# Three empty places in the order of the attention units of an attention-and-FFN kernel

## The chip, the core and the metric

One core of one Trainium2 chip runs the whole program. The metric is the device time of one execution in microseconds (us); the figure that counts is the median of several runs. Five engines work side by side, each in the order of its own instruction stream: PE (TensorE, matrix products; PEld is its loading of weights), DVE (VectorE), ACT (ScalarE), POOL (GpSimd) and SP (SyncE, which here only issues transfers). They wait for one another through semaphores, and a waiting instruction holds up everything behind it on its engine.

## What is computed

Causal attention in a window of 128 positions, with a linear bias for each head, for 8 batches of 8 heads, 576 positions and head size 64; and on its result, taken as 4608 tokens of 512 values, a feed-forward network with a sigmoid gate.

```python
scores = scale * np.matmul(q, k.transpose(0, 1, 3, 2))
scores = np.where(mask, scores + bias[None], -1000000000.0)
attn = np.exp(scores - np.max(scores, axis=-1, keepdims=True))
attn = attn / (np.sum(attn, axis=-1, keepdims=True) + 1e-09)
x = np.matmul(attn, v).transpose(0, 2, 1, 3).reshape(B * S, H * D)
h = x @ w_in
g = h * (1.0 / (1.0 + np.exp(-1.702 * h)))
return g @ w_out
```

## The kernel before

**Attention** is cut into units of one pair of heads and up to 256 queries. Batches 0 and 1 are cut "whole": three sections of 256, 256 and 64 queries, each with four units, one for a pair of heads. That makes 12 units for each of these two batches. Batches 2 to 7 have 20 units each, of a finer form. The list `units` holds all of them in order, and a *tick* moves the pipeline on by one place: in tick n the unit at place n gets its scores (`scores`, PE, L324 for the whole units), the one at n-1 its bias and minimum (`biased`, DVE, L351), its exponents (`exponents`, ACT, L374) and its normalization (`normal`, DVE L392 and L393 for the reciprocal, then L402 on POOL or DVE and L399 on ACT), the one at n-2 its transposition (`flip`, PE L419 and copies on ACT and DVE, L427), and the one at n-3 its product with v (`mix`, PE L476, copied out at L485 into the tile of tokens `x` or `xf`). A tick also loads a later unit's q and k through SP.

**The FFN** works on chunks of 256 tokens, 18 of them, each in 16 steps, one for each 128 of the 2048 hidden values. A step is `up` (12 products into `h_ps`, L552: the high part `xh` of the tokens with both parts of the weights, then the low part `xl` with the high part), a chain over ACT (L557, tanh), DVE (L558), ACT (L561, `gh`) and POOL (L562, `gl`), and `down` (6 products into `acc`, L571). Chunk 0 runs its first 8 steps, then chunk 1 its 16, then chunk 0 the rest, then chunks 2 to 17. At the start of a chunk `split_x` (L536, L538) makes `xh` on ACT and `xl` half on POOL and half on DVE.

**The weights** come as 64-bit words and are decoded once, in 32 halves (a `w_in` and a `w_out` half for each of the 16 steps): L211 on ACT, L212 and L213 on DVE, L216 on ACT for the high part, L217 on POOL for the low part. All of it happens beside the first FFN steps. In the names below `w_7_925` is a decoded half of step 7: the smaller last number is its `w_in` half.

**What sets the order.** The first 7 ticks run before the first FFN step. After that a planner in the main loop gives each FFN step a share of a tick: for each entry of `due` (so many units must be done when such a chunk begins) it divides the ticks still to go by the steps still to go, and takes the largest quotient (`pace`). Chunk 0 starts at step 0, chunk 1 at step 8, chunk 2 at step 32. In the kernel before, `due` begins with 4, 8, 12 and 16 units for the chunks 0, 1, 2 and 2 (chunk 2 holds the last 64 tokens of batch 0 and the first 192 of batch 1). Over the program order that comes of this, a scheduler then sets each engine's stream by its own simulated times, so an instruction can stand earlier or later on its engine than the loop wrote it.

The units that the change touches are the third section of batch 0 (64 queries, `64x192` in the rows), at places 8 to 11, and what follows them, the first section of batch 1 (`128x128` and `128x256` in the rows).

Of the kernel before, what the change touches and what calls it, by code (L numbers as in the profile page):

```python
# [32 lines left out]
BIG = 3.0e38  # L33
FAR = 1.0e37
DEPTH = 3
BESIDE = range(4)
WB = 2
DECODE_TICKS = 5, 6, 7
# [65 lines left out]
def whole_batch(b):  # L104
    units = []
    for hp in range(NP):
        blocks = pair_blocks(hp)
        n = len(blocks)
        chunks = [Chunk(i * P, P, [(blocks[i], P)] + [(z, 0) for z in blocks[i + 1:i + 2]]) for i in range(n)]
        for i in range(0, n, 3):  # L110
            Segment(i * P, 3 * P, P if i + 3 < n else 0, chunks[i:i + 3])
        done = 0
        for i in range(0, n, 2):
            upto = min(i + 1, n) if i + 2 < n else n
            units.append(Unit(b * NP + hp, blocks[i:i + 2], chunks[i:i + 2], chunks[done:upto]))
            done = upto
    return units
# [20 lines left out]
def part_batch(b, lo, hi):  # L138
    return [WholeUnit(b, hp, lo, hi) for hp in range(NP)]
# [3 lines left out]
def tile_kernel(ctx: ExitStack, tc: tile.TileContext, q0, k0, v0, qT, kT, v, w_in, w_out, out):  # L143
# [103 lines left out]
    def load_whole(u):  # L247
        if u.at == DEPTH:

            u.rq = ffn.tile([P, 2 * P], F32, name="rq", tag="g")  # L250
            u.rk = ffn.tile([P, 2 * P], F32, name="rk", tag="gh")
            u.rv = ffn.tile([P, 2, 2, D], F32, name="VV", tag="gl")
        else:
            u.rq = raw.tile([P, 2 * P], F32, name="rq", tag="rq")
            u.rk = raw.tile([P, 3 * P], F32, name="rk", tag="rk")
        move(u.rq[:, :u.hi - u.lo], q0[u.pair, :, u.lo:u.hi])
        if u.early:
            tc.keep_in_program_order(nc.scalar.dma_start(u.rk[:, :u.hi - u.k0], k0[u.pair, :, u.k0:u.hi]))
        else:
            move(u.rk[:, :u.hi - u.k0], k0[u.pair, :, u.k0:u.hi])  # L260

    def load_whole_v(u):
        if u.at != DEPTH:
            u.rv = att.tile([P, 3, 2, D], F32, name="VV", bufs=3)
        full = (u.hi - u.k0) // P
        end = u.k0 + full * P
        move(u.rv[:, :full], v0[u.pair, u.k0:end].rearrange("(c p) h d -> p c h d", p=P))
        if end < u.hi:
            move(u.rv[:u.hi - end, full], v0[u.pair, end:u.hi])
# [262 lines left out]
    def split_x(c, x):  # L532
        xh = xp.tile([P, NC, T], F32R, name="xh")
        xl = xp.tile([P, NC, T], F32R, name="xl")
        for k in range(NC):
            (nc.scalar.copy if c in BESIDE else nc.vector.tensor_copy)(xh[:, k], x[:, k])  # L536
            sub = nc.vector if k % 2 else nc.gpsimd
# [54 lines left out]
    units, due = [], []  # L592
    for b in range(B):
        start = max((b * S + S - 1) // T - XBUFS, 0)
        if b < WB:
            for lo, hi in ((0, 2 * P), (2 * P, 4 * P), (4 * P, S)):
                units += part_batch(b, lo, hi)
                due.append((len(units), (b * S + lo) // T, start))
        else:
            units += whole_batch(b)  # L600
            due.append((len(units), b * S // T, start))
    for n, u in enumerate(units):
        u.at = n
        u.early = n < due[0][0]
    units += [None] * 4
    loads = [u for u in units if u]
    ticks = 0
# [115 lines left out]
def build(nc, arrays):  # L723
    args = []
    for name, a in arrays.items():
        args.append(nc.dram_tensor(name, a.shape, mybir.dt.from_np(a.dtype), kind="ExternalInput").ap())
    args.append(nc.dram_tensor("out", (NT, DM), F32, kind="ExternalOutput").ap())
    with tile.TileContext(nc, schedule_with_timeline_sim=True) as tc:
        tile_kernel(tc, *args)
# [44 lines left out]
```

## Time and profile before

| | |
|---|---|
| median of 3 runs | 1064.5 us (1063.76 to 1065.91) |
| the profiled execution | 1068.36 us |
| its span, from the first to the last instruction | 1066.3 us |
| mean granted PE clock over the span | 0.995 of full speed |
| moved from and to HBM | 67.63 MB read, 9.44 MB written, 72 GB/s over the span |
| chain of work that ended last, by engine | PE 94%, DVE 3%, ACT 1%, DMA 1%, issue 1% |

The span is cut into stretches below; "busy" is the time in which an engine worked on an instruction, and a row with a number in brackets at its end tells how long the engine had stood idle before the instruction, and what it had waited for. A PE product is counted busy until its result is out, so two products that follow each other closely overlap: what a product costs PE is the distance between starts, which is smaller than its duration.

### The profile page before, as it was taken

What the parts mean: (1) busy time and instruction counts of PE and PEld (TensorE: products, weight loads), DVE (VectorE), ACT (ScalarE), POOL (GpSimd) and SP (SyncE); (2) the same over time, 40 slices, a digit from 0 to 9 for tenths busy, and PEclk for the clock granted to TensorE, in tenths of its full rate; (3) what the DMA queues carried; (4) which work ended last, traced back from release to release, by engine and by line L of the source; (5) the groups of instructions that cost most, each with busy time, mean ns of one, the idle gap of its engine ahead of it and who ended that gap; (6) DMA issues with size and microseconds to landing.
All of it is one profiled execution on the core that took longest, in us unless ns stands there. A gap on an engine that the chain in (4) does not pass through costs nothing.

```text
span 1066.3 us, 21362 instructions
## 1 busy us (share of the span) xinstructions
PE 1052.9 (99%) x7041; PEld 929.1 (87%) x7041; DVE 660.5 (62%) x2117; ACT 597.2 (56%) x1811; POOL 603.5 (57%) x863
## 2 busy tenths in 40 slices
PE   9899999999999999999999999999999999999998
PEld 5567787889989999999999999999999999998987
DVE  6797522568887777545767668767877687313121
ACT  6879853466666565535555556655665656322222
POOL 4579933567676666554656557656666665323232
PEclk9899999999999999999999999999999999999999
DMA  8872001223222132102121223212222221000000
GB/s 307 281 261 73 25 22 56 73 67 96 75 76 81 51 102 67 57 14 71 54 79 52 71 62 91 66 60 78 79 63 85 57 78 28 20 2 20 1 21 20
DMA packets 88109, 78.45 MB, mean 74 GB/s; under 512 B 36800, under 2 KB 79296, under 8 KB 88000
## 3 DMA queue, kind: packets, MB, share of 16 engines
q1 hardware_dynamic: 82240, 67.14, 21.4%
q10 hardware_dynamic: 5760, 9.96, 2.6%
q8 instruction: 55, 0.90, 0.3%
q14 instruction: 54, 0.44, 0.1%
HBM read 67.63 MB, written 9.44 MB: 72 GB/s over the span
## 4 chain that ended last, share of the span: by engine, by line
PE 94%; DVE 3%; ACT 1%; DMA 1%; issue 1%; POOL 0%; SPq 0%; DVEq 0%; POOLq 0%; ACTq 0%
PE h_ps L552 38%; PE acc L571 37%; PE s_ps L334 5%; PE x_ps L499 5%; PE t_ps L442 4%; PE x_ps L476 2%; PE t_ps L419 1%; PE sb_ps L324 1%; PE s_ps L324 1%; DVE wc L213 1%; DMA rw<-w_out 1%; ACT pb L374 1%; DVE rec L392 0%; PE acc L189 0%; DVE rw L212 0%
## 5 line engine op out<-in xcount | busy, mean ns | idle before, releaser
L562 POOL TENSOR_TENSOR gl<-g,gh 128x256 fp32r<-128x256 f32 x288 | 218.0, 757 | 292.2 <-ACT gh L561 224.9
L552 PE MATMUL h_ps<-xh,w 128*128 128x256 f32 x2304 | 370.2, 284 | 1.1 <-POOL w L217 0.6
L552 PEld LDWEIGHTS h_ps<-xh,w 128*128 128x128 f32 x2304 | 328.5, 189 | 34.5 <-issue 2.8
L571 PE MATMUL acc<-w,gh 128*128 128x512 f32 x1152 | 324.9, 400 | 0.0
L558 DVE SCALAR_TENSOR_TENSOR g<-g,h_ps 128x256 f32<-128x256 f32 x288 | 119.6, 415 | 207.9 <-ACT g L557 206.5
L557 ACT ACTIVATE g<-h_ps 128x256 f32<-128x256 f32 x288 | 110.4, 383 | 229.4 <-PE h_ps L552 207.3
L571 PEld LDWEIGHTS acc<-w,gh 128*128 128x128 f32 x1152 | 196.5, 189 | 27.9 <-ACT g L557 0.3
L552 PE MATMUL h_ps<-xl,w 128*128 128x256 f32 x1152 | 194.6, 280 | 0.0
L561 ACT CAST gh<-g 128x256 fp32r<-128x256 f32 x288 | 116.9, 406 | 129.5 <-DVE g L558 121.1
L571 PE MATMUL acc<-w,gl 128*128 128x512 f32 x576 | 188.0, 401 | 0.0
L552 PEld LDWEIGHTS h_ps<-xl,w 128*128 128x128 f32 x1152 | 164.2, 188 | 6.0
L312 POOL TENSOR_TENSOR K<-rk,K 128x384 fp32r<-128x384 f32 (+1 forms) x120 | 109.0, 909 | 65.2 <-ACT Q L292 15.9
L381 ACT ACTIVATE pb<-pb,mins 128x256 f32<-128x256 f32 (+2 forms) x216 | 104.9, 487 | 43.8 <-DVE mins L362 40.1
L571 PEld LDWEIGHTS acc<-w,gl 128*128 128x128 f32 x576 | 92.6, 188 | 9.5 <-issue 0.9
L311 POOL TENSOR_TENSOR Q<-rq,Q 64x256 fp32r<-64x256 f32 (+1 forms) x120 | 83.1, 692 | 22.2 <-DVE K L310 4.9
L406 DVE TENSOR_SCALAR pb<-pb,rec 128x256 f32<-128x256 f32 (+2 forms) x216 | 91.8, 461 | 3.2
L362 DVE CUSTOM_DVE_ANT_0 pb<-s_ps,bias 128x256 f32<-128x256 f32 (+3 forms) x240 | 85.7, 377 | 4.1 <-PE s_ps L334 2.8
L392 DVE TENSOR_SCALAR rec<-sums 128x2 f32<-128x2 f32 (+3 forms) x144 | 48.5, 336 | 58.4 <-ACT pb L381 53.6
L334 PE MATMUL s_ps<-K,Q 128*128 128x256 f32 (+1 forms) x432 | 79.8, 289 | 0.4 <-DVE mins L362 0.4
L310 DVE CAST K<-rk 128x384 fp32r<-128x384 f32 (+1 forms) x120 | 52.5, 438 | 41.2 <-PE s_ps L334 34.2
L461 DVE TENSOR_TENSOR pl<-t_ps,ph 128x512 fp32r<-128x512 f32 (+2 forms) x120 | 72.2, 604 | 9.3 <-ACT ph L455 6.6
L442 PE MATMUL t_ps<-ident,pb 128*128 128x128 f32 x408 | 74.2, 272 | 0.0
(68 smaller groups left out, 1322.2 us busy)
## 6 DMA issues: line engine op xcount, KB each, us to landing
rk<-kT SPq DMA_DIRECT2D x72, 192.0 KB, 2.5
rq<-qT SPq DMA_DIRECT2D x96, 128.0 KB, 2.3
out<-o ACTq DMA_DIRECT2D x36, 256.0 KB, 2.1
rw<-w_in SPq DMA_DIRECT2D x16, 512.0 KB, 6.5
rw<-w_out SPq DMA_DIRECT2D x16, 512.0 KB, 7.0
rk<-kT SPq DMA_DIRECT2D x48, 128.0 KB, 2.2
rv<-v SPq DMA_DIRECT2D x96, 64.0 KB, 1.9
rq<-q SPq DMA_DIRECT2D x16, 128.0 KB, 2.6
```

The lines of the kernel that those rows point to most:

```text
L312: nc.gpsimd.tensor_tensor(K2, rk, K1.bitcast(F32), ALU.subtract)
L334: nc.tensor.matmul(u.s[:b.rows, e, b.first:b.end], u.Q[:, b.q0 - u.q0:b.q0 - u.q0 + b.rows], k[:, ko:ko + b.end - b.first], start=(z == 0) ...
L362: nc.vector.tensor_tensor_reduce(b.p[ra:rb, cs:b.end], u.s[ra:rb, e, cs:b.end], bias[head][ra:rb, cs:b.end], -SCALE, BIG, ALU.add, ALU.min ...
L381: nc.scalar.activation(live, live, AF.Exp, bias=u.mins[:b.rows, e:e + 1], scale=-1.0, accum_out=u.sums[:b.rows, e:e + 1],)
L406: nc.vector.tensor_scalar(live, live, u.rec[:rows, e:e + 1], None, ALU.mult)
L442: nc.tensor.transpose(u.t[:c.n, w:w + b.rows], b.p[:b.rows, col:col + c.n], ident[:b.rows, :b.rows])
L552: nc.tensor.matmul(h, w1[f][:, z, k * P:(k + 1) * P], x[:, k], start=(n == 0), stop=(n == len(ops) - 1))
L557: nc.scalar.activation(g, h, AF.Tanh, scale=0.851)
L558: nc.vector.scalar_tensor_tensor(g, g, 1.0, h, ALU.add, ALU.mult)
L561: nc.scalar.copy(gh, g)
L562: nc.gpsimd.tensor_tensor(gl, g, gh.bitcast(F32), ALU.subtract)
L571: nc.tensor.matmul(acc, g[:, t * P:(t + 1) * P], w2[f][:, z], start=(f == self.f0 and n == 0), stop=(f == self.f1 - 1 and n == 2))
```

## The change

Three empty places (`None`) are put into `units` behind the eighth unit, that is between the second and the third section of batch 0. Ticks pass over them without work. The counts in `due` behind them grow by 3: they begin with 4, 8, 15 and 19 where they were 4, 8, 12 and 16.

```diff
+GAP = 3
...
                 units += part_batch(b, lo, hi)
                 due.append((len(units), (b * S + lo) // T, start))
+                if len(due) == 2:
+                    units += [None] * GAP
...
     for n, u in enumerate(units):
-        u.at = n
-        u.early = n < due[0][0]
+        if u:
+            u.at = n
+            u.early = n < due[0][0]
```

Ticks 7 to 10 fall into the FFN steps 1 to 4 in both kernels, at a pace of 4/5 of a tick for a step. Before, they brought the scores of the eighth unit and of the first three units of the third section; now they bring the eighth unit's alone, and the pipeline runs empty. From step 5 on the pace is 8/24 of a tick for a step before and 11/24 now, and tick 18 before, tick 21 now, both in step 28, score the same unit. From step 32 on the program order is the same again. No instruction is added or taken out; the decoding of weights keeps its places in the program.

How the streams come out: the first place is POOL, from the last decoding for step 6 to the `xl` of chunk 1. Before:

```order
L217 TENSOR_TENSOR w_6_842<-wc,w_6_842 128x512
L402 TENSOR_SCALAR pb<-pb,rec 128x128
L402 TENSOR_SCALAR pb<-pb,rec 128x256
L217 TENSOR_TENSOR w_7_925<-wc,w_7_925 128x512
L562 TENSOR_TENSOR gl<-g,gh 128x256
L217 TENSOR_TENSOR w_7_932<-wc,w_7_932 128x512
L562 TENSOR_TENSOR gl<-g,gh 128x256
L402 TENSOR_SCALAR pb<-pb,rec 128x128
L402 TENSOR_SCALAR pb<-pb,rec 128x256
L217 TENSOR_TENSOR w_8_1013<-wc,w_8_1013 128x512
L538 TENSOR_TENSOR xl<-xf,xh 128x256 x2
```

The same place now (lines of the changed kernel are one higher up to the list of units, and four higher behind it):

```order
L218 TENSOR_TENSOR w_6_827<-wc,w_6_827 128x512
L563 TENSOR_TENSOR gl<-g,gh 128x256
L403 TENSOR_SCALAR pb<-pb,rec 64x192
L218 TENSOR_TENSOR w_7_886<-wc,w_7_886 128x512
L218 TENSOR_TENSOR w_7_893<-wc,w_7_893 128x512
L563 TENSOR_TENSOR gl<-g,gh 128x256
L218 TENSOR_TENSOR w_8_942<-wc,w_8_942 128x512
L539 TENSOR_TENSOR xl<-xf,xh 128x256 x2
```

Two pairs of normalizations of the first section of batch 1 (`128x128` with `128x256`) have gone behind the `xl`; one of the third section of batch 0 (`64x192`), which stood further ahead before, is here now.

The second place is PE, from the last attention work ahead of chunk 1 to that chunk's first product with `xl`. Before:

```order
L476 MATMUL x_ps<-pw,VV 64x256
L476 MATMUL x_ps<-pw,VV 64x128 x2
L552 MATMUL h_ps<-xh,w_0_387 128x256
L324 MATMUL s_ps<-rk,rq 128x128
L552 MATMUL h_ps<-xh,w_0_387 128x256
L419 MATMUL t_ps<-ident,pb 128x128
L552 MATMUL h_ps<-xh,w_0_387 128x256
L419 MATMUL t_ps<-ident,pb 128x128
L552 MATMUL h_ps<-xh,w_0_387 128x256 x5
L552 MATMUL h_ps<-xh,w_1_525 128x256 x8
L419 MATMUL t_ps<-ident,pb 128x128 x3
L552 MATMUL h_ps<-xl,w_0_387 128x256 x2
```

Now:

```order
L325 MATMUL s_ps<-rk,rq 128x128
L325 MATMUL sb_ps<-rk,rq 128x128
L325 MATMUL s_ps<-rk,rq 128x256
L325 MATMUL sb_ps<-rk,rq 128x256
L420 MATMUL t_ps<-ident,pb 128x64
L420 MATMUL t_ps<-ident,pb 64x64
L572 MATMUL acc_621<-w_6_827,gl 128x512
L572 MATMUL acc_622<-w_6_827,gl 128x512
L553 MATMUL h_ps<-xh,w_0_387 128x256 x3
L325 MATMUL s_ps<-rk,rq 128x128
L553 MATMUL h_ps<-xh,w_0_387 128x256 x5
L553 MATMUL h_ps<-xl,w_0_387 128x256 x2
```

Counted from the start of the stream to the first product with `xl` of chunk 1, PE has these fewer instructions ahead of it: 4 scores `128x128` and 4 `128x256` (two units of batch 1), 12 transpositions `128x128` and two smaller ones, 12 mix products `64x64` (three units of batch 0), 2 `64x256` and 2 `64x128` (the mix of one unit of batch 1), and the 8 products of the next step (`w_1`). All of them have gone behind it. The scores of the first unit of batch 1, which stood singly among other work before, stand here in one run.

The third place is DVE, between the two decodings for step 8 and the `xl` of chunk 1. Before:

```order
L213 SCALAR_TENSOR_TENSOR wc<-wc,rw_8_565 128x512
L212 TENSOR_SCALAR rw_15_1077<-rw_15_1077 128x512
L392 TENSOR_SCALAR rec<-sums 128x4
L393 RECIPROCAL rec<-rec 128x4
L213 SCALAR_TENSOR_TENSOR wc<-wc,rw_8_567 128x512
L351 ISA pb,mins<-s_ps,bias_78 128x128
L351 ISA pb,mins<-s_ps,bias_78 128x256
L351 ISA pb,mins<-sb_ps,bias_79 128x128
L351 ISA pb,mins<-sb_ps,bias_79 128x256
L538 TENSOR_TENSOR xl<-xf,xh 128x256 x2
```

Now:

```order
L214 SCALAR_TENSOR_TENSOR wc<-wc,rw_8_565 128x512
L213 TENSOR_SCALAR rw_15_1006<-rw_15_1006 128x512
L214 SCALAR_TENSOR_TENSOR wc<-wc,rw_8_567 128x512
L214 SCALAR_TENSOR_TENSOR wc<-wc,rw_9_583 128x512
L539 TENSOR_TENSOR xl<-xf,xh 128x256
```

(The short rows that read out the minimum behind each L351 are left out.) Three units of batch 1, four L351 each, stood ahead of the first `xl` and now stand behind it, with two pairs of L392 and L393; one decoding more stands ahead of it.

## The prediction

> **What bounds the kernel now.** I read the busy times of the whole page first, then the busy times by stretch, then PE's own rows with their waits in the one stretch where it waits.
>
> ```profile
> PE 1052.9 (99%) x7041; PEld 929.1 (87%) x7041; DVE 660.5 (62%) x2117; ACT 597.2 (56%) x1811; POOL 603.5 (57%) x863
> ```
>
> PE is busy for 99% of the span. So the end can move only by time in which PE waits or runs slowly; PE's work itself is the same in both kernels. Where does it wait? By stretch (busy us of PE, PEld, DVE, ACT, POOL, with the number of instructions, then granted clock and DMA):
>
> ```profile
> 32.44:61.72 29.28, 24.71 (x138) 16.72 (x138) 24.64 (x65) 22.90 (x68) 17.11 (x15) 0.83 0.85 295
> 61.72:93.32 31.60, 29.77 (x204) 21.79 (x201) 29.30 (x65) 27.98 (x92) 27.65 (x25) 0.99 0.49 166
> 93.32:126.38 33.06, 33.06 (x208) 25.22 (x207) 18.92 (x59) 32.51 (x95) 30.50 (x28) 1.00 0.18 51
> 126.38:192.88 66.50, 66.50 (x411) 51.82 (x410) 18.14 (x56) 31.31 (x99) 27.54 (x34) 1.00 0.13 38
> ...
> 400.00:1057.00 657.00, 656.94 (x4447) 602.14 (x4446) 389.69 (x1252) 328.66 (x983) 349.33 (x529) 1.00 0.18 52
> ```
>
> The rows begin at the tanh of the FFN steps 0, 3, 8, 16 and 32. Up to about 93 us DVE is nearly full (29.30 of 31.60), ACT and POOL not far behind, and PE has gaps: here the weights are decoded beside attention. From 93 us to 126 us ACT is full (32.51 of 33.06), but PE has no gap any more. Behind that PE alone is full. So the last place at which anything but PE sets the time lies before 93 us. The waits of PE there, from where the two streams first differ (about 50 us):
>
> ```profile
> 52.88 0.74 PE L552 MATMUL h_ps<-xh,w 128*128 128x256 f32 x4 [0.60 <-POOL w L217]
> ...
> 57.33 0.30 PE L419 MATMUL t_ps<-ident,pb 64*128 64x64 f32 x2 [1.11 <-DVE mins L351]
> ...
> 71.59 0.27 PE L419 MATMUL t_ps<-ident,pb 64*128 64x64 f32 x1 [0.77 <-DVE mins L351]
> ...
> 78.68 0.74 PE L552 MATMUL h_ps<-xh,w 128*128 128x256 f32 x4 [0.52 <-ACT w L216]
> ...
> 82.11 0.44 PE L419 MATMUL t_ps<-ident,pb 128*128 128x128 f32 x2 [0.40 <-POOL pb L402]
> ```
>
> 0.60 + 1.11 + 0.77 + 0.52 + 0.40 = 3.40 us: two waits for a decoded weight, three for attention work that the change moves. In two stretches PE also ran at half clock:
>
> ```profile
> 34.87:38.28 3.41, 1.85 (x10) 1.20 (x11) 2.86 (x12) 3.39 (x12) 0.63 (x1) 1.00 0.87 314
> 38.28:45.11 6.83, 6.83 (x27) 4.30 (x24) 4.92 (x11) 5.14 (x15) 5.01 (x5) 0.50 0.61 185
> ...
> 55.35:58.76 3.41, 2.30 (x14) 1.27 (x13) 3.41 (x8) 2.49 (x9) 2.04 (x2) 1.00 0.84 240
> 58.76:62.18 3.42, 3.42 (x19) 2.82 (x20) 3.30 (x9) 3.08 (x10) 1.79 (x2) 0.50 0.99 354
> ...
> 69.00:72.42 3.42, 2.65 (x24) 1.68 (x22) 3.42 (x7) 2.26 (x10) 2.05 (x2) 1.00 0.68 180
> ```
>
> The first lies ahead of the change. The second, 58.76 to 62.18, can have cost at most half of its 3.42 us, 1.7. **All that the change could win is therefore 3.4 + 1.7 = 5.1 us.**
>
> **The change part by part.** What the program moves: the third section of batch 0 and, behind it, the units of batch 1 leave the stretch before 93 us and come back by FFN step 28 (about 175 us), where ACT and POOL are busy for less than half of the time (31.31 and 27.54 of 66.50); the moved ACT, DVE and POOL work is hidden there by PE, and I cost it at nothing. If that cover were gone, ACT's part of some 5 us would show. The SP queue issues the same loads; two weight pairs now stand ahead of one unit's q and k. Their landing is no wait of PE in the rows above, and the unit is needed later than before: nothing.
>
> The place that decides is the first product with `xl` of chunk 1 (FFN step 8). Ahead of it all three side engines lose work, and so does PE. I set the one against the other.
>
> *What comes earlier.* POOL:
>
> ```profile
> 79.78 2.27 POOL L402 TENSOR_SCALAR pb<-pb,rec 128x128 f32<-128x128 f32 x2 [0.67 <-DVE rec L393]
> ...
> 86.57 1.94 POOL L402 TENSOR_SCALAR pb<-pb,rec 128x128 f32<-128x128 f32 x2
> 88.47 1.27 POOL L217 TENSOR_TENSOR w<-wc,w 128x512 fp32r<-128x512 f32 x1
> 89.70 2.07 POOL L538 TENSOR_TENSOR xl<-xf,xh 128x256 fp32r<-128x256 f32 x2
> ```
>
> Both pairs of L402 go behind the `xl`: 2.27 + 1.94 = 4.2 us. DVE:
>
> ```profile
> 77.30 0.68 DVE L213 SCALAR_TENSOR_TENSOR wc<-wc,rw 128x512 int32<-128x512 int32 x1
> ...
> 84.65 1.26 DVE L392 TENSOR_SCALAR rec<-sums 128x4 f32<-128x4 f32 x1
> ...
> 86.04 1.09 DVE L213 SCALAR_TENSOR_TENSOR wc<-wc,rw 128x512 int32<-128x512 int32 x1
> 87.05 0.28 DVE L351 CUSTOM_DVE_ANT_0 pb<-s_ps,bias 128x128 f32<-128x128 f32 x1
> ...
> 88.16 1.86 DVE L538 TENSOR_TENSOR xl<-xf,xh 128x256 fp32r<-128x256 f32 x2
> ```
>
> One unit's four L351 take 88.16 - 87.05 = 1.11 us, three units 3.3. Of the two pairs L392 and L393 one took 86.04 - 84.65 = 1.39; undisturbed it is about 0.3, so both are 1.7. One L213 more stands ahead, 0.68 when undisturbed. Together 4.3 us. ACT:
>
> ```profile
> 88.02 0.84 ACT L399 ACTIVATE pb<-pb,rec 128x128 f32<-128x128 f32 x2
> ...
> 89.22 0.45 ACT L374 ACTIVATE pb<-pb,mins 128x128 f32<-128x128 f32 x1
> ...
> 90.99 0.34 ACT L485 COPY xf<-x_ps 128x192 f32<-128x192 f32 x1
> ```
>
> Two units' exponents at 90.99 - 89.22 = 1.77, two L399 at 0.84, and some ten short copies, less one L211: about 5 us.
>
> If the three queues ran wholly side by side, the `xl` would come 4.2 to 5 us earlier. If DVE and POOL took turns, it would be 4.2 + 4.3 = 8.5. How much they do so is in two rows, the group of the L213 in this stretch (count, busy us, mean ns) and the busy times of the stretch:
>
> ```profile
> L213 DVE SCALAR_TENSOR_TENSOR wc<-wc,rw 128x512 int32<-128x512 int32 x15 | 18.6, 1239 | 1.2 <-ACT wc L211 1.2
> ```
>
> ```profile
> 50.00:93.00 43.00, 39.47 (x261) 28.83 (x260) 40.67 (x89) 37.28 (x120) 36.05 (x31) 0.96 0.62 214
> ```
>
> Between 50 and 94 us an L213 took 1239 ns on the mean, against 680 undisturbed: 15 x 0.56 = 8.4 us of waiting inside instructions, while POOL worked for 36.05 of 43 us, so about a quarter of POOL's time was paid on DVE too. I take 6 us, nearer the lower end.
>
> The Trainium skill has a rule for this (SBUF — State Buffer, Who interferes with whom): VectorE and GpSimd share one pair of ports, and for some instructions, those with two SBUF inputs among them, the later to start blocks until the other is done. The trace agrees for L213, by the row just shown (1239 against 680 ns). By that rule in its hardest form the sum below would use 8.5, which is the second rival.
>
> *What is put behind it on PE.* The counts stand with the second place of the order above; the prices are distances between starts:
>
> ```profile
> 82.48 0.49 PE L324 MATMUL s_ps<-rk,rq 64*128 64x128 f32 x2
> 82.90 0.60 PE L476 MATMUL x_ps<-pw,VV 128*64 128x64 f32 x8
> 83.42 0.55 PE L419 MATMUL t_ps<-ident,pb 128*128 128x128 f32 x3
> 83.73 0.71 PE L552 MATMUL h_ps<-xh,w 128*128 128x256 f32 x4
> ...
> 86.24 0.37 PE L324 MATMUL sb_ps<-rk,rq 64*128 64x128 f32 x1
> ...
> 87.09 0.65 PE L476 MATMUL x_ps<-pw,VV 128*64 128x256 f32 x2
> 87.67 0.74 PE L571 MATMUL acc<-w,gl 128*128 128x512 f32 x2
> ...
> 88.45 0.86 PE L476 MATMUL x_ps<-pw,VV 128*64 128x256 f32 x6
> 89.24 0.38 PE L552 MATMUL h_ps<-xh,w 128*128 128x256 f32 x1
> ...
> 92.32 1.18 PE L552 MATMUL h_ps<-xl,w 128*128 128x256 f32 x8
> ```
>
> A unit's scores: 82.90 - 82.48 = 0.42 and 87.09 - 86.24 = 0.85, so 1.27, two units 2.5. Twelve `64x64` products at 0.52 for four: 1.6. Thirteen transpositions' worth at 0.31 / 3: 1.3. The mix of a unit of batch 1: 87.67 - 87.09 = 0.58 and 89.24 - 88.45 = 0.79, so 1.4. Eight FFN products: the row at 92.32 has eight in 1.18 until the last result is out, so 1.0 of PE's time. Sum 7.8 us, still to be done behind the `xl`.
>
> *The sum.* Before, the `xl` was ready on POOL at 89.70 + 2.07 = 91.77, and PE used it at 92.32: PE had 0.55 us to spare. Now PE, with less ahead of it, reaches the place first and waits for the `xl`. The end moves by +7.8 (work behind) - 6.0 (earlier) - 0.55 = +1.25 us. Off that goes the scores of one unit that now stand in one run, two products at a time: I put 0.6 of its 1.27. That leaves about +0.6 us. Against the profiled execution (1068.36 us, span 1066.3) it gives 1069.0; that execution lay 3.9 above the median of the runs shown, so against the median it is 1064.5 + 0.6 = **1065.1 us**: no difference that a measurement of this kernel could tell, which is about 0.2%, 2.1 us.
>
> **The rivals.** *The waits of PE vanish* (faster). Three of the five waits, 1.11 + 0.77 + 0.40 = 2.3 us, end at attention work that leaves, and if the one at 57.33 goes, the slice before 58.76 is fuller and the half clock behind it need not come, 1.7 more: 4.0 us, 1060.5. For it: DVE is the fullest engine there and gets less to do. Against it: by the order each place on PE next waits for a decoded weight, and two of the five waits are that already.
>
> *DVE and POOL take turns.* With 8.5 in place of 6.0 the sum is -1.9 us, 1062.6. Against it: only a quarter of it is seen.
>
> *PE cools for want of filling* (slower). Attention is what PE does while weights are decoded. The clock fell after slices with 1.85 and 2.30 us of PE work, and stayed with 2.65 (69.00 to 72.42). That slice ends in transpositions and scores, from 71.59 on, that now come later: 72.42 - 71.59 = 0.8 of its 2.65 us. Below about 2.3 the clock halves for the next 3.41 us, which costs up to 1.7. With the `xl` only 4.2 us earlier as well, the end moves by 7.8 - 4.2 - 0.55 - 0.6 + 1.7 = +4.1, 1068.6. It decides from the point where such a slice has under 2.3 to 2.65 us of work.
>
> The Trainium skill (TensorE: Matmul & The Clock Gate, Part 1: The HAM clock gate) lets the clock fall only after a window of some 3.4 us without work; by it this rival would cost nothing for the clock. The trace differs: it fell after slices that were 54% and 67% busy, so I keep the rival.
>
> *The order hardly changes.* The scheduler may draw the late units forward again, as it does with some `64x192` rows, and PE's total is the same: 1064.5.
>
> **How the numbers follow.** Forecast 0.42; waits vanish 0.15; turns 0.18; cooling 0.17; hardly a change 0.08. Faster by over 0.2%: the first rival, half of the second, a little of the forecast's edge, 0.27. Slower: cooling and the forecast's upper edge, 0.25. Within: 0.48. The range goes from the first rival to the cooling, 1060.3 to 1068.9; beyond stand a win of all 5.1 us, and two cooled slices.
>
> **What would show it.** PE's row for the first `xl` product of chunk 1 should have a wait in brackets, near 86 us in place of 92.3, and the L402 of the `128x128` units should stand behind it. The tanh of step 16, before at 126.4 us, should come some 6 to 7 us earlier, with as much attention still to do, and that of step 32 at 192.9 within 2 us. I am wrong in size if the `xl` comes before 84 or after 88 us, and in mechanism if PE waits at other places behind 93 us, say for `gl`, or if the granted clock has a third stretch at a half.

## The result, and the profile after

The changed kernel is slower: 1077.59 us (median of 4 runs, 1076.37 to 1078.53) against 1064.17 us (median of 4 runs, 1063.76 to 1065.91), ratio 1.0122, 95% interval 1.0105 to 1.0140. That is 13.4 us more; 0.6 us were forecast, and the range ended at 1068.9.

The page of the changed kernel, busy times of the whole span (its profiled execution took 1076.37 us, span 1074.3):

```profile
PE 1056.8 (98%) x7041; PEld 930.5 (87%) x7041; DVE 664.1 (62%) x2117; ACT 595.9 (55%) x1811; POOL 603.0 (56%) x863
```

The same stretches as before the prediction (busy us of PE, PEld, DVE, ACT, POOL with instructions, granted clock, DMA):

```profile
61.72:93.32 31.60, 26.32 (x151) 20.57 (x150) 28.57 (x47) 23.88 (x69) 27.53 (x24) 0.89 0.26 83
93.32:126.38 33.06, 33.06 (x217) 25.80 (x216) 19.81 (x49) 27.96 (x84) 29.71 (x28) 1.00 0.16 47
126.38:192.88 66.50, 66.50 (x410) 52.71 (x410) 20.47 (x74) 33.98 (x106) 22.75 (x29) 1.00 0.14 43
...
400.00:1057.00 657.00, 656.92 (x4453) 602.44 (x4452) 394.72 (x1270) 331.86 (x995) 352.14 (x535) 1.00 0.19 53
```

Between 62 and 93 us PE did 151 products in place of 204, and at a lower clock (0.89 in place of 0.99). DVE did 47 instructions in place of 65 and was still busy for 28.57 us (29.30 before). From 93 us on the rows look alike, and yet more than half of the loss lies there. To see it one has to cut at the same FFN steps, not at the same microseconds. The trace of the kernel before that the prediction used lost 3.7 us ahead of the change, so the comparison is with a second trace of it (first experiment). Stretches from the tanh of FFN step 0 to that of 8, 32, 40, 62 and 66, the kernel before:

```profile
31.67:89.57 57.90, 51.42 (x340) 36.43 (x340) 55.08 (x128) 50.54 (x159) 44.87 (x39) 0.97 0.69 240
89.57:189.15 99.58, 99.58 (x618) 77.07 (x617) 37.15 (x114) 63.84 (x194) 58.09 (x61) 1.00 0.15 42
189.15:216.43 27.28, 27.28 (x185) 23.20 (x184) 14.44 (x47) 12.80 (x48) 14.55 (x21) 1.00 0.27 78
216.43:300.62 84.19, 84.19 (x595) 77.82 (x593) 69.01 (x231) 58.65 (x178) 58.31 (x90) 1.00 0.28 77
300.62:315.98 15.36, 14.96 (x107) 13.46 (x106) 14.06 (x42) 8.11 (x26) 10.80 (x18) 1.00 0.30 81
```

and the changed one:

```profile
32.28:87.36 55.08, 46.97 (x272) 33.51 (x271) 51.37 (x106) 43.42 (x126) 44.09 (x35) 0.91 0.65 232
87.36:182.52 95.16, 94.92 (x597) 75.47 (x596) 39.33 (x115) 61.52 (x187) 54.09 (x58) 1.00 0.13 38
182.52:222.87 40.35, 40.35 (x259) 30.05 (x258) 11.76 (x47) 20.68 (x75) 16.11 (x23) 1.00 0.26 73
222.87:306.62 83.75, 83.75 (x593) 76.98 (x592) 68.18 (x235) 56.44 (x180) 58.02 (x91) 1.00 0.30 82
306.62:327.83 21.21, 18.69 (x128) 16.01 (x127) 20.50 (x71) 13.74 (x45) 15.68 (x24) 1.00 0.40 115
```

After minus before, in us: -2.82, -4.42, +13.07, -0.44, +5.85, together +11.24; with 0.6 at step 0 this is all of the difference of the two spans (11.8). The opening does 68 PE records less and becomes only 2.8 us shorter. The missing work is made up at steps 32 to 40 (74 records more, +13.1 us), and at steps 62 to 66 21 records more take 5.9 us, since there DVE is full (20.50 of 21.21) and PE waits.

Since work moves between the stretches, I use a second measure: **lost time of PE**, the length of a stretch less the price of each product in it. The price of a shape is the median distance between the ends of that product and of the one ahead of it, over the traces from 60 us on (0.118 us for 128x256, 0.233 for 128x512, 0.109 for 128x128, 0.06 to 0.22 for the small f32 ones). It is worked out, no row of a view. By it the second trace of before lost 11.3 us in steps 0 to 8, 1.7 in 32 to 40 and 1.0 in 62 to 66; the changed kernel 16.1, 4.4 and 4.4. The differences, **4.8 + 2.7 + 3.4 us**, with 0.4 at step 0 and -0.3 at steps 8 to 32, are 11.0 of the 11.8; the rest is spread over the other steps. How the 2.4 us at steps 8 to 40 divide depends on the price: with one for each tile and shape, in place of one for each shape, they are 0.7 at steps 8 to 32 and 1.7 at 32 to 40.

PE's rows with the longest waits from 60 us to step 8 in the changed kernel:

```profile
63.98 0.74 PE L553 MATMUL h_ps<-xh,w 128*128 128x256 f32 x4 [1.10 <-ACT w L217]
...
72.17 0.33 PE L420 MATMUL t_ps<-ident,pb 64*128 64x64 f32 x2 [1.58 <-DVE mins L352]
...
81.57 0.37 PE L325 MATMUL sb_ps<-rk,rq 64*128 64x128 f32 x1 [0.85 <-ACT pw L428]
...
84.73 0.49 PE L325 MATMUL s_ps<-rk,rq 64*128 64x128 f32 x2 [1.08 <-DVE mins L352]
```

The second trace of before has there only two waits above 0.5 us, both for weights:

```profile
61.52 0.74 PE L552 MATMUL h_ps<-xh,w 128*128 128x256 f32 x4 [0.95 <-POOL w L217]
...
74.94 0.74 PE L552 MATMUL h_ps<-xh,w 128*128 128x256 f32 x4 [0.51 <-ACT w L216]
```

And the slices at half clock in the changed kernel, each behind the slice ahead of it:

```profile
42.02:45.43 3.41, 2.21 (x13) 1.05 (x11) 2.54 (x9) 3.41 (x11) 1.64 (x2) 1.00 1.01 395
45.43:48.84 3.41, 3.41 (x17) 2.37 (x18) 2.77 (x7) 2.19 (x7) 3.41 (x3) 0.50 1.02 416
62.50:65.91 3.41, 1.88 (x12) 1.24 (x11) 3.41 (x6) 2.60 (x8) 2.91 (x3) 1.00 0.98 345
65.91:69.32 3.41, 3.41 (x17) 2.47 (x16) 3.38 (x6) 2.15 (x6) 3.11 (x3) 0.50 0.45 130
69.32:72.73 3.41, 1.83 (x11) 1.22 (x11) 3.41 (x8) 1.13 (x3) 2.13 (x3) 1.00 0.32 91
72.73:76.15 3.42, 3.42 (x13) 3.00 (x13) 3.37 (x7) 3.25 (x11) 2.72 (x3) 0.50 0.00 0
```

Three slices (10.2 us) ran at half clock; in the second trace of before it was one (3.4 us), in the first three as well.

### The profile page after: what moved, and what is told of

Its sections match the earlier page's. It is cut to its first block, busy times and chain, and to the rows that moved or that the text cites. A ratio compares the mean times of both kernels' runs of the same rounds, so it can differ in the third digit from the quotient of the medians.

```text
span 1074.3 us, 21369 instructions
## 1 busy us (share of the span) xinstructions
PE 1056.8 (98%) x7041; PEld 930.5 (87%) x7041; DVE 664.1 (62%) x2117; ACT 595.9 (55%) x1811; POOL 603.0 (56%) x863
## 4 chain that ended last, share of the span: by engine, by line
PE 93%; DVE 4%; DMA 1%; ACT 1%; issue 1%; SPq 0%; POOL 0%; DVEq 0%; POOLq 0%; ACTq 0%
PE h_ps L553 37%; PE acc L572 37%; PE s_ps L335 5%; PE x_ps L500 5%; PE t_ps L443 4%; PE x_ps L477 2%; DVE wc L214 1%; PE t_ps L420 1%; PE s_ps L325 1%; PE sb_ps L325 1%; DVE rw L213 1%; DMA rw<-w_out 1%; PE acc L190 1%; ACT pb L375 0%; SPq L156 0%
## 5 line engine op out<-in xcount | busy, mean ns | idle before, releaser
L393 DVE TENSOR_SCALAR rec<-sums 128x2 f32<-128x2 f32 (+3 forms) x144 | 45.6, 317 | 60.4 <-ACT pb L382 49.7
L311 DVE CAST K<-rk 128x384 fp32r<-128x384 f32 (+1 forms) x120 | 48.8, 407 | 41.2 <-PE s_ps L335 35.7
```

## The experiments

Each ratio is against runs of the kernel before on the same chip. "Half clock" is the time up to 105 us at a granted clock of 0.5, from windows of 0.5 us. The last columns are lost time of PE by FFN steps in the profiled execution, which is one run and can lie off the median. In e2, e6 and e11 one more slice at half clock lies within steps 62 to 66. In e10, e12, e14 and e15 `GAP` is 0, so that there are no empty places.

| kernel | median us | ratio (95%) | half clock us | 0-8 | 8-32 | 32-40 | 62-66 |
|---|---|---|---|---|---|---|---|
| before, first trace | 1064.17 | 1 | 10.2 | 14.6 | 4.8 | 1.7 | 1.0 |
| before, second trace | 1065.6 (1 run) | | 3.4 | 11.3 | 4.9 | 1.7 | 1.0 |
| changed | 1077.59 | 1.0122 (1.0105-1.0140) | 10.2 | 16.1 | 4.6 | 4.4 | 4.4 |
| e2 batch 2 paced earlier | 1077.32 | 1.0117 (1.0090-1.0144) | 20.5 | 21.6 | 5.3 | 4.4 | 5.2 |
| e3 chunk 2's units 3 steps earlier | 1083.32 | 1.0179 (1.0153-1.0205) | 3.4 | 19.1 | 7.9 | 5.4 | 2.2 |
| e4 one empty place | 1079.35 | 1.0141 (1.0119-1.0163) | 10.2 | 16.1 | 8.0 | 4.5 | 2.1 |
| e5 chunk 2's units 12 steps earlier | 1079.34 | 1.0144 (1.0121-1.0168) | 20.5 | 22.9 | 8.6 | 3.9 | 1.1 |
| e6 gap at batch 2 | 1068.22 | 1.0033 (1.0018-1.0047) | 0 | 10.8 | 4.9 | 1.8 | 5.0 |
| e7 gap at batch 1 | 1072.22 | 1.0080 (1.0059-1.0101) | 10.2 | 15.5 | 7.1 | 3.0 | 1.0 |
| e8 changed, scaling on ACT | 1076.73 | 1.0108 (1.0088-1.0128) | 3.4 | 12.3 | 7.1 | 3.8 | 2.1 |
| e9 changed, low part on DVE | 1082.91 | 1.0168 (1.0147-1.0188) | 20.5 | 23.0 | 6.2 | 4.4 | 2.2 |
| e10 before, low part on DVE | 1065.17 | 1.0006 (0.9995-1.0017) | 6.8 | 9.1 | 5.7 | 2.4 | 1.1 |
| e11 changed, fillers | 1077.90 | 1.0121 (1.0104-1.0139) | 3.4 | 10.7 | 5.3 | 4.3 | 3.6 |
| e12 before, fillers | 1070.20 | 1.0059 (1.0042-1.0077) | 3.4 | 10.9 | 6.7 | 1.7 | 1.1 |
| e13 gap of 5 in batch 1 | 1066.16 | 1.0005 (0.9993-1.0018) | 10.2 | 13.7 | 4.9 | 1.1 | 1.5 |
| e14 before, scaling on ACT | 1066.18 | 1.0006 (0.9997-1.0016) | 0 | 11.3 | 4.3 | 0.9 | 2.0 |
| e15 before, half of the low parts on DVE | 1068.48 | 1.0038 (1.0021-1.0056) | 17.1 | 15.6 | 4.6 | 3.4 | 1.0 |

### The kernel before once more

No edit.

> The kernel before, unchanged, for a second trace of it: its first profiled execution lay 3.9 us above the median of its runs. If that was chance, this one takes 1063.5 to 1066 us, and the tanh of FFN step 8 or that of step 64 comes some 4 us earlier than in the first trace (93.32 and 315.56 us), which says which stretch carries the rest of the 13.4 us between the kernels. If a profiled execution of this kernel is always longer, it takes 1068 again.

It took 1065.6 us with a span of 1062.5, 3.8 less than the first trace's. At the tanh of step 8 the second trace is 3.8 us ahead (89.57 against 93.32), at the last tanh too. So the first trace was 3.8 us long, all of it ahead of the change, where it had two half-clock slices that the second lacks.

### Pacing, and the number of empty places

```diff
+SLACKS = {4: 5}     # e2;  {2: 5} in e3;  {2: 12} in e5
...
-            pace = max(pace, (n + 3 - ticks - credit) / max(starts[by] - 1 - SLACK - now, 1))
+            pace = max(pace, (n + 3 - ticks - credit) / max(starts[by] - 1 - SLACKS.get(by, SLACK) - now, 1))
```

> Three empty places, but batch 2's units (due by chunk 4) are paced to be done three FFN steps earlier; up to FFN step 38 as the changed kernel. Theory A (attention runs a unit late from step 33 on, and chunk 4 at steps 63 and 64 has to wait for it, 5.5 us): the waits at steps 63 and 64 go, 1072 us. Theory B (all is lost ahead of step 8, by waits of PE and slices at half clock; what is seen later is only the same work elsewhere): 1077.6 us.

> Three empty places, but the units due by chunk 2 (the third section of batch 0) are paced to be done three FFN steps earlier, so that less is left to catch up in steps 33 to 38, and batch 2 begins less late. Ahead of step 8 the streams are those of the changed kernel. Theory A: 1072 us or a little under. Theory B: 1077.6 us.

The fourth kernel has `GAP = 1`. (Where the expectations count mix products short at step 8, each of those f32 products leaves two records in the trace: 32 there.)

> One empty place in place of three. At FFN step 8 PE's stream is as far short of attention as with three (16 mix products, 8 scores, 9 transpositions), at steps 33 to 38 too; but at step 64 nothing is left in arrears. Theory A: the loss at steps 63 and 64 is smaller or gone, 1072 to 1074 us. Theory B: the place at step 8 is the same, 1077.6 us. A loss that grows with each empty place by the same amount would give 1068.6 us.

> Three empty places; the units due by chunk 2 are paced to be done twelve FFN steps earlier. Up to step 12 PE's stream is that of the changed kernel, from step 24 on what was short is made up (6 mix products short of before, not 16), and batch 2 begins as early as before. Theory C (three places pay: about 5.0 us of PE's time lost ahead of step 8, 2.9 at steps 32 to 40 and 3.4 at 63 to 66, the last two because attention runs late): 1063.7 + 5 = 1069 us. Theory D (the loss ahead of step 8 decides, and what comes later is the same whatever is late): 1076 us or more.

None came down: 1077.32, 1083.32, 1079.35 and 1079.34 us. So theory A, that the waits at steps 62 to 66 carry most, fell: with one place, or with everything made up by step 40, those lost 2.1 and 1.1 us there in place of 4.4, and were no faster. One empty place costs what three cost: at step 8 PE's stream lacks the same work. Made up earlier (e3, e5), the work costs more at steps 8 to 32, 7.9 and 8.6 us in place of 4.6. Theory C's 1069 us for e5 fell too, and theory D's 1076 or more came: what is not paid at 62 to 66 was paid at steps 8 to 32. e2's streams are the changed kernel's up to step 35, those of e3 and e5 up to step 6, and their openings still lost between 19.1 and 22.9 us in their traces, against 16.1.

### The gap at other places

```diff
-                if len(due) == 2:
+                if len(due) == 6:     # e6;  3 in e7;  4 with GAP = 5 in e13
                     units += [None] * GAP
```

> The three empty places stand behind batch 1 instead of behind the eighth unit. PE's stream is that of before up to step 32; from step 44 to 62 batch 2 is a unit late (6 mix products, 8 scores), as in the changed kernel. Theory C: only the loss at steps 63 to 66 is there, some 1 to 3.4 us, 1065 to 1067 us. Theory D: nothing is lost, 1063.7 us.

1.0033 (1.0018 to 1.0047), 3.5 us by the ratio: theory D's 1063.7 us fell, and theory C's range was a little low. The opening is that of before, and steps 62 to 66 alone differ:

```profile
300.00:319.85 19.85, 17.76 (x108) 15.41 (x107) 19.18 (x59) 11.71 (x39) 13.91 (x23) 0.91 0.36 101
```

108 PE records, against 107 in the last row of before above, take 19.85 us in place of 15.36; DVE is busy for 19.18 of them, with 59 instructions in place of 42. **The late unit costs 3.5 us there, near the changed kernel's 3.4 of lost time.** The two are not quite alike: in this trace PE also ran a slice at half clock there (0.91 on the mean; 1.00 in the changed kernel), so of the 4.0 us that it lost more than before up to 1.7 can be the clock's.

> Five empty places behind the first section of batch 1. PE's stream is that of before up to step 36 within a unit, at steps 44 to 56 it is 5 to 6 mix products short as in the run with the gap at batch 2, but at step 62 nothing is short. If the 3.5 us of that run come from what is still short when chunk 4 is begun (steps 62 to 64), this one takes the time of before, 1064 to 1065 us. If being late between steps 44 and 56 is what costs, it takes 1068 us.

1.0005 (0.9993 to 1.0018): late at steps 44 to 56, but with nothing short at step 62, it costs nothing that can be measured. What counts is what is still to do when chunk 4 must begin.

This run also shows what the clock does in the opening. Up to step 8 its streams are those of before, and by chance its trace ran as long at half clock as the changed kernel's, 10.2 us:

```profile
32.00:92.02 60.02, 53.80 (x338) 38.61 (x337) 53.16 (x128) 51.12 (x159) 45.74 (x40) 0.91 0.68 231
```

It lost 13.7 us there, the changed kernel 16.1. **So at an equal clock 2.4 of the opening's 4.8 us remain.** Whether the change brings the rest, more time at half clock, is not shown: four traces of before's opening (both of before, e6 and e13) had 10.2, 3.4, 0 and 10.2 us of it. Of the whole difference the clock decides little: at a mean granted clock of 1.000 the kernel before took 1063.49 to 1065.56 us (11 runs), and e2 1076.18 (1 run).

> The three empty places stand behind the third section of batch 0. Up to step 5 PE's stream is nearly that of before, at step 8 it is 4 mix products short instead of 16, and from step 20 on nothing is short. Theory C: a part of the loss ahead of step 8 by the work that is missing there (2.3 of 3.8 us by a fixed price for each product) and none later: 1064 to 1067 us. Theory D: as the changed kernel, if a delay anywhere ahead of step 8 does it: 1076 us.

1.0080 (1.0059 to 1.0101), 8.5 us by the ratio, more than expected, though at step 8 only 8 records of mix products are missing in place of 32, and nothing is lost at 62 to 66. Its trace lost 4.2 us more than the second trace of before in the opening, with 10.2 us at half clock (1.8 more than e13, which has as much), 2.2 more at steps 8 to 32 and 1.3 more at 32 to 40. The loss is not in proportion to the work that leaves.

### Fillers for PE

```diff
+            if self.c == 0 and 0 < f < F0:
+                for _ in range(6):
+                    nc.tensor.matmul(h, w1[f - 1][:, 0, :P], self.xh[:, 0], start=True, stop=True)
             ops = [(z, x, k) for z, x in ((0, self.xh), (1, self.xh), (0, self.xl)) for k in range(NC)]
```

> The changed kernel with six more products of 128x256 ahead of each of the FFN steps 1 to 7, with weights that are there already and a result that is written over: 42 of about 0.12 us, 5.0 us, as much as the attention that left. If the granted clock halves because PE is short of work (half-clock time up to 105 us: 10.2, 20.5, 3.4 and 20.5 us in four traces of this opening, 3.4, 10.2 and 0 in three of before's), the half-clock time falls below 7 us and the time by 1 to 4 us, 1074 to 1076. If not, the fillers cost up to 5 us, 1077 to 1083.

> The same fillers in the kernel before. They replace nothing there: 1064 us if PE waits anyway where they stand, 1064 to 1069 if it doesn't; a fall below 1063 would say that the kernel before, too, loses time to the clock.

The opening (steps 0 to 8) of the changed kernel with fillers, and apart from it that of before with fillers:

```profile
31.58:88.42 56.84, 50.88 (x324) 38.01 (x321) 47.71 (x109) 45.56 (x129) 44.70 (x37) 0.97 0.64 225
```

```profile
31.98:90.68 58.70, 53.37 (x359) 39.85 (x358) 53.57 (x120) 48.05 (x147) 45.45 (x38) 0.97 0.66 228
```

In the kernel before, 42 products of 0.118 us (5.0 us) cost 1.0059 (1.0042 to 1.0077), 6.3 us: there PE has no time for them. (Not all of it is their own time: they also push attention back, since at step 8 this stream is short of 8 records of mix products, as with the gap at batch 1, and it lost 1.8 us more than before at steps 8 to 32.) In the changed kernel they cost nothing, 1077.90 against 1077.59. **So the changed opening holds 5 us in which PE waits or runs at half clock.** That the attention that left had been done for nothing in such time fits this: by the prices the stretch holds 46.6 us of work in the second trace of before and 39.0 in the changed kernel, 7.6 less, and became only 2.8 us shorter. With the fillers the half-clock time is 3.4 us, as in the second trace of before, and the lost time of the opening falls from 16.1 to 10.7, close to before's 11.3. The expected fall of 1 to 4 us didn't come: what fillers win, they take.

### POOL's work elsewhere

```diff
-            engines = "PPVA" if u.early else "PAPA"
+            engines = "PPVA" if u.early else "AAAA"     # e8, e14
...
-        pin(nc.gpsimd.tensor_tensor(res[:, 1], w, res[:, 0].bitcast(F32), ALU.subtract))
+        pin(nc.vector.tensor_tensor(res[:, 1], w, res[:, 0].bitcast(F32), ALU.subtract))     # e9, e10; in e15 for w1 alone
```

> The changed kernel with all scalings of the weights by the reciprocals on ACT from the second section on, so that POOL loses some 8 instructions of 1.1 us ahead of step 8, and ACT, which had become freer there, gains them. If the loss ahead of step 8 is DVE standing in its decode instructions while POOL works (a lone L214 takes 0.68 us, there up to 3.40), then L213 and L214 of the decode take less and the time falls by 2 to 5 us, 1073 to 1075 us. If PE is short of work there whatever DVE does, it stays at 1077.

> The changed kernel with the decode's last step (the low part, L218) on DVE instead of POOL, so that DVE does 32 more instructions of about 0.68 us in the opening stretch and POOL none of 1.27 us or more. If the product with xl of chunk 1 doesn't come earlier because DVE stands in its decode instructions while POOL works, then L213 and L214 take 0.34 and 0.68 us, step 8 comes 5 us or more ahead of the changed kernel's and the time falls to 1070 to 1074 us. If DVE is bound by its own work there, it has 11 us more of it ahead of step 8 and the time rises to 1082 or more.

> The same edit in the kernel before (no empty places). If standing behind POOL costs DVE more than the instruction does: 1060 to 1062 us, faster than before; if DVE is bound by its own work: 1068 us or more.

> The kernel before with all scalings on ACT from the second section on, the control of the same edit in the changed kernel. If the opening is bound by DVE standing behind POOL, the tanh of step 8 comes 3 to 5 us earlier than at 89.6 us and the time falls to 1061 to 1063 us; if ACT, which is full there, is next, it stays at 1064 to 1066.

> The kernel before with the low part of the weights into the FFN on DVE and of those out of it on POOL, half of the edit that moved all of them. With all, step 8 came 5.4 us earlier with 2.3 us of attention less ahead of it, and nothing was left of it at the end. With half, 1.0 us is short at step 8. If standing behind POOL is what the opening loses, 1061 to 1063 us; if the freed time always goes to work that has to be done later, 1064 to 1065.

DVE does stand in its decode instructions while POOL works. Two rows of DVE in the changed kernel:

```profile
67.29 3.15 DVE L213 TENSOR_SCALAR rw<-rw 128x512 int32<-128x512 int32 x1
...
76.68 3.40 DVE L214 SCALAR_TENSOR_TENSOR wc<-wc,rw 128x512 int32<-128x512 int32 x1
```

Their groups in steps 0 to 8 (count, busy us, mean ns, idle ahead), in the second trace of before (where the line numbers are one lower), in the changed kernel and in e9:

```profile
L213 DVE SCALAR_TENSOR_TENSOR wc<-wc,rw 128x512 int32<-128x512 int32 x18 | 19.1, 1063 | 1.2 <-ACT wc L211 1.2
L212 DVE TENSOR_SCALAR rw<-rw 128x512 int32<-128x512 int32 x26 | 18.7, 727 | 1.5 <-DMA rw<-w_out 1.1 <-DMA rw<-w_in 0.4
```

```profile
L213 DVE TENSOR_SCALAR rw<-rw 128x512 int32<-128x512 int32 x26 | 22.2, 864 | 3.0 <-DMA rw<-w_in 1.6 <-DMA rw<-w_out 1.4
L214 DVE SCALAR_TENSOR_TENSOR wc<-wc,rw 128x512 int32<-128x512 int32 x18 | 20.1, 1124 | 0.4 <-ACT wc L212 0.4
```

```profile
L213 DVE TENSOR_SCALAR rw<-rw 128x512 int32<-128x512 int32 x27 | 12.4, 458 | 3.0 <-DMA rw<-w_in 3.0
L214 DVE SCALAR_TENSOR_TENSOR wc<-wc,rw 128x512 int32<-128x512 int32 x17 | 11.9, 707 | 5.2 <-ACT wc L212 5.2
```

From the changed kernel to e9, 864 to 458 and 1124 to 707 ns: the standing is gone, as expected; and e9 is slower (1.0168). That is the time that was expected if DVE is bound by its own work (1082 or more), but with 20.5 us at half clock its trace doesn't show that this is the cause. e8 brought step 8 to 84.41 us (87.36 in the changed kernel), but its 1076.73 us isn't told apart from 1077.59. In the kernel before, e10 brought step 8 5.4 us earlier and gave it all back by step 36, where it was 16 records of mix products short; e14 made no difference, e15 was slower. e10 and e15 met none of the times expected for them; e14 came close to the 1064 to 1066 us expected if ACT is the next to be full. DVE's standing is real, but freeing DVE won nothing in five tries. No kernel here beats the one before.

## Why the prediction was wrong

- **What bounds the kernel.** Right that PE sets the time, and that up to 93 us it has gaps. Wrong that "behind that PE alone is full": at steps 62 to 66 DVE is busy for 14.06 of 15.36 us even before, PE waits for it as soon as a unit comes late, and that place lay outside the stretches that I read. 
- **The xl of chunk 1, the deciding place.** The first product with it:

```profile
88.58 1.18 PE L552 MATMUL h_ps<-xl,w 128*128 128x256 f32 x8
```

```profile
85.83 0.40 PE L553 MATMUL h_ps<-xl,w 128*128 128x256 f32 x2
```

  The second trace of before comes first, the changed kernel behind it. By the trace that I used (92.32) it came 6.5 us earlier, near the forecast 86 us; but 3.7 of these were a disturbance of that trace ahead of the change, so that the agreement was luck. Like with like it is 88.58 - 85.83 = 2.75 us. **This is the first term that was mis-sized: 6.0 us, measured 2.75.** By my own sum, 7.8 - 2.75 - 0.55 - 0.6 = +3.9; the lost time of the opening gives 4.8. The engines' savings that I added up didn't all come: in steps 0 to 8 POOL, of which I expected 4.2 us, is busy for only 0.8 us less; DVE, of which I expected 4.3, has 22 instructions less (106 in place of 128) and is busy for 3.7 us less, while its decode instructions stand for longer (means of 864 and 1124 ns in place of 727 and 1063). Nor did the wait show at the xl, but at `mins` and weights.
- **PE cools for want of filling (rival, 0.17).** Its sign came, its cause isn't shown. Three slices ran at half clock, behind slices with 2.21, 1.88 and 1.83 us of PE work, and the condition that I gave for a wrong mechanism, a third stretch at half clock, is met. Against the one slice of the second trace of before, 6.8 us at half speed can account for up to 3.4 of the 4.8 us; against e13, with as much half clock as the changed kernel, 2.4 of the 4.8 remain. But the first trace of before had three such slices too, so the change need not have brought them. Nor is the border sharp that I put at 2.3 to 2.65 us: of 41 slices with 1.55 to 2.46 us of PE work only 17 were followed by one at half clock (last section). The rule of the Trainium skill (TensorE: Matmul & The Clock Gate, Part 1: The HAM clock gate), which has the clock fall after a window without work, would have left out this loss; no slice here was empty, and the trace decides.
- **Moved work costed at nothing behind 93 us.** **This step failed**, with 2.7 us at steps 32 to 40 and 3.4 at 62 to 66. The work was to be back by step 28; in PE's stream it was not: against the second trace of before, 32 records of mix products are missing ahead of the tanh of step 8, 42 ahead of that of step 28, 44 at 32 and 8 at 38. I had taken its return from the program order, and the scheduler's streams differ from it. I asked whether ACT and POOL were free over 126.38 to 192.88, and they were; I didn't ask what the units still owed at step 32 do to those behind them. The tanh of step 32 was forecast within 2 us; it came at 182.52, 6.6 us ahead of the second trace of before, because the attention had not been done yet: it came at steps 32 to 40, in 13.1 us. From there on batch 2 runs about a unit late up to step 62 (4 to 8 records of mix products), and then chunk 4 must begin. PE's rows there in the changed kernel:

```profile
317.22 0.74 PE L335 MATMUL s_ps<-K,Q 128*128 128x256 f32 x4 [0.43 <-DVE mins L363]
318.20 0.36 PE L500 MATMUL x_ps<-ph,VV 128*128 128x256 f32 x1 [0.25 <-DVE xf L530]
...
319.90 0.86 PE L553 MATMUL h_ps<-xh,w 128*128 128x256 f32 x5 [0.82 <-DVE xh L537]
...
324.09 0.48 PE L335 MATMUL s_ps<-K,Q 128*128 128x256 f32 x2 [0.65 <-POOL K L313]
```

  and what DVE has to do for the wait at 319.90:

```profile
317.29 0.77 DVE L530 TENSOR_TENSOR xf<-x_ps,xb 64x192 f32<-64x192 f32 x3
318.08 1.29 DVE L588 TENSOR_SCALAR o<-acc 128x512 f32<-128x512 f32 x2
...
319.56 0.28 DVE L537 CAST xh<-xf 128x256 fp32r<-128x256 f32 x1
```

  Mixes of the last pair of heads of batch 2 give `xf` at 317.29, DVE then writes chunk 3's output, and only behind that the last quarter of `xh`, on which the next chunk waits. The run with the gap at batch 2 has its loss at this place alone.
- **The loss at steps 32 to 40** (2.7 us) stays argued: PE is busy all the time there, at clock 1.00. The reading of its rows is that f32 products of attention, in twos between FFN products, cost more each than in runs; no kernel here tried that alone. It can't be all: the 16 records of `64x192` scores, which stand in twos, take 3.7 us here and took 3.7 us at steps 8 to 32 in the second trace of before.
- **DVE and POOL taking turns (rival).** Seen in the durations, but freeing DVE moved no time. The rule of the Trainium skill (SBUF — State Buffer, Who interferes with whom), by which a VectorE instruction with two SBUF inputs contends with a GpSimd instruction that reads SBUF, agrees with L214, 1124 ns beside POOL and 707 without most of it; it told nothing of the time.
- **The size.** 4.8 + 2.7 + 3.4 + 0.4 - 0.3 = 11.0 of the 11.8 us between the two spans. The medians are 13.4 apart; the profiled execution of the changed kernel was the lowest of its four, and the second trace of before lay 1.4 us above the median of 1064.17. Why the work costs as much when it is made up at steps 8 to 32 (e3 to e5) stays open.

## What to carry to other kernels

Work that fills an engine's waits is free where it stands, and costs its full price wherever that engine is full: ahead of a move, ask what the engine does in the time that it leaves, and test it with fillers, which tell in two runs whether a stretch has time to spare, as far as they leave the order of the rest alone. Cut two traces at the same step of the program, not at the same microsecond, and look at every later place where the moved stream has a deadline; in e13, being late cost nothing that could be measured ahead of such a place. Take a second trace of the kernel before, ahead of building a sum on the first.

## What the runs showed of the hardware

The granted clock falls without an empty slice. In fourteen of these traces, cut into their slices of 3.41 us from about 31 to 105 us, each of the 8 full-clock slices with under 1.55 us of PE work was followed by one at half clock, none with 2.47 us or more, and of the 41 between them 17; what decides between these stays open. How long an opening runs at half clock differs between runs of one order: 10.2 and 20.5 us in the changed kernel and e2, whose streams agree up to step 35, and 10.2, 3.4, 0 and 10.2 us in four traces of before's. Runs of one kernel differ with it: e2 took 1075.47 and 1076.18 us at a mean granted clock of 0.998 and 1.000, and 1083.82 at 0.989.
